# Stores of the first two batches in two pieces, and the last leftover block copied by one engine

## The chip, the cores and the metric

The kernel runs on one core of a Trainium2 chip. The metric is device time in microseconds (us): 236.17 us, the median of three runs (236.04 to 236.21). The engines are named as in the profile: PE is TensorE, DVE is VectorE, ACT is ScalarE, POOL is GpSimd, and SP is SyncE, which here issues DMAs (transfers) and waits. DMAs are issued on three queues, those of SP, ACT and POOL.

## The reference

Attention over 32 learned memory slots in each of 8 batches and 8 heads (576 tokens, head size 64), followed by a gated feed-forward block over the 4,608 tokens. Cut to what matters:

```python
a = softmax(phi)                                  # over the tokens, 8 x 8 x 576 x 32
k_m, v_m = einsum("bhsm,bhsd->bhmd", a, k), einsum("bhsm,bhsd->bhmd", a, v)
x = softmax(q @ k_m.T / sqrt(64)) @ v_m           # 8 x 8 x 576 x 64
x = x.transpose(0, 2, 1, 3).reshape(4608, 512)
out = (silu(x @ w_gate) * (x @ w_val)) @ w_out    # d_ff = 1536, out is 4608 x 512 in float32
```

## The kernel before

**Tiling.** The batches are taken one after the other, the first two interleaved. For a batch the kernel forms the memory's keys and values, the normalised attention `t_A`, and `t_U`, the product of the memory's values with the gate and value weights. The hidden layer `t_h` then comes from `t_U` and `t_A` (line 508), with the SiLU on ACT (line 525) and the gating product on DVE (line 531).

The last matmul, hidden layer by `w_out`, is done per batch on 2 x 2 blocks with seven products in place of eight (`products`, line 681; the matmul itself is line 719). Of the 576 tokens of a batch it takes 512, as two groups of 256: group `n` of a batch holds every second token (`out_r`, line 65). The sums and differences of blocks that the seven products need are `t_S` and `t_Q` (POOL and DVE) and `t_T` (of the weights). The remaining 64 tokens of each batch, the leftover, are gathered for four batches at a time (`quad`), which makes one small problem of 2 x 2 blocks of 128 tokens by 256 columns.

**Results and stores.** The four blocks of a result are called c11, c12, c21 and c22. PE accumulates products in PSUM banks; ACT moves intermediate sums to SBUF (`keep`, line 740: `t_p`, `t_q`); DVE adds (line 749). For a batch:

- `c11` and `c12` (lines 756 and 766) fill the tile `o1`, the first group's 256 tokens x 512 columns, held as 128 partitions x 2 x 512; `c22` and `c21` (lines 762 and 771) fill `o2`, the second group's.
- `both` calls `store_block` (line 671), which issues one DMA on SP's queue: 256 tokens, 512 KB.
- The tiles `o1` and `o2` come from a pool of three buffers (tag `to`), so the fourth tile waits for the landing of the first one's store.

For the leftover, `leftover` (line 777) makes one block of 128 tokens x 256 columns: for c11, c22 and c12 DVE adds (line 789); for c21 the bank is only copied. The block holds 64 tokens of each of two batches, and so has two stores of 64 KB (`store_leftover`, line 677), the first on SP's queue. For the second quad, which ends the kernel (`end` is true), the second store goes on SP's queue for c11, on ACT's for c22, on POOL's for c12 and on ACT's for c21, and the copy of c21 is cut in two halves of 128 columns, one on DVE and one on ACT (lines 793 and 794).

**Order.** The program is written by hand (`manual_schedule`, line 62): each engine and each queue does its work in the order in which the code names it. The end of the kernel is the list of the second quad's products, in the order p1/c11, q6, p5, c22, c12, c21 (line 822), each followed at once by its operation. In PE's last 1.5 us these are the product for c22, the one for c12 and the one for c21, six matmuls each. After that there is only the program's closing part, which the profile puts at line 1108: SP waits for all semaphores, and all engines meet in a barrier.

**Waits.** The framework that builds the program gives each DMA of SP's and ACT's queues one of eight semaphores in turn, and each DMA of POOL's queue one of eight others. A DMA waits for the one that had its semaphore before it. An instruction that waits for more semaphores than it can name itself has waiting rows (events) ahead of it.

Of the kernel before, what the change touches and what calls it, by code (L numbers as in the profile page):

```python
# [14 lines left out]
def kernel(  # L15
# [19 lines left out]
    nc = tc.nc  # L35
# [29 lines left out]
    out_r = out.rearrange("(b t r) c -> b r t c", b=B, r=2)  # L65
# [15 lines left out]
    def done(*tiles):  # L81

        for t in tiles:
            free.append(held.pop(id(t))[0])
# [243 lines left out]
    def copy(eng, out, in_):  # L328
        if eng == "a":
            nc.scalar.copy(out=out, in_=in_)  # L330
        else:
            nc.vector.tensor_copy(out=out, in_=in_)
# [337 lines left out]

    def store_block(t_o, b, n, cols):

        nc.sync.dma_start(
            out=out_r[b, n, 0:256, cols].rearrange("(u t) c -> t u c", u=2), in_=t_o[:, :, cols]
        )

    def store_leftover(t_o, b, cols, eng):

        eng.dma_start(out=out_b[b, 512:S, cols], in_=t_o)

    def products(b, by_hand, quad=None):

        h = DM // 2
# [3 lines left out]
        end = quad == 1 or (quad is None and b + 1 == B)  # L687
# [65 lines left out]
        def both(name, t0, cols):  # L753
            store_block(mine[name], b, t0 // 256, cols)
# [20 lines left out]
            both("o2", 256, slice(0, DM))  # L775

        def leftover(name, room, half, cols):
            other = dict(c22=nc.scalar, c12=nc.gpsimd, c21=nc.scalar) if end else {}
            engs = (nc.sync, other.get(name, nc.sync))

            def run():
                if room:
                    t = mine[room, "all"][:, half]
                else:
                    t = work.tile([128, h], FP32, tag="to", name="t_o")
                home = mine[dict(c11="a", c12="c").get(name, "s")]
                other = dict(c11="p1", c22="p5", c12="q6").get(name)
                if other:
                    nc.vector.tensor_tensor(
                        out=t, in0=home[:, 0], in1=mine[other][:, 0], op=ALU.add  # L790
                    )
                elif end:
                    copy("v", t[:, 0:h // 2], home[:, 0, 0:h // 2])
                    copy("a", t[:, h // 2:h], home[:, 0, h // 2:h])
                else:
                    copy("a", t, home[:, 0])
                if name != "c22":
                    done(home)
                for k in range(2):
                    x = 4 * quad + 2 * (name > "c20") + k  # L800
                    store_leftover(t[64 * k:64 * k + 64], x, cols, engs[k])

            return run
# [3 lines left out]
            c11=c11, c22=c22, c12=c12, c21=c21,  # L807
        )
        if quad is not None:
            ops.update(  # L810
                c11=leftover("c11", None, 0, lo), c12=leftover("c12", "q6", 1, hi),
                c22=leftover("c22", "p5", 1, hi), c21=leftover("c21", "q6", 0, lo),
            )
# [299 lines left out]
```

## Time and profile before

| | |
|---|---|
| median of the runs | 236.17 us (236.04 to 236.21) |
| the profiled execution | 236.21 us |
| its span, first to last instruction | 234.3 us |
| PE busy | 223.9 us (96%) |
| DVE, ACT, POOL busy | 183.1, 173.9, 141.1 us |
| granted TensorE clock | 1.00 throughout |
| DMA traffic | 36.84 MB, mean 157 GB/s |
| last matmul ends | 229.54 us |
| last DMA is issued | 230.24 us |

The span is what the trace shows; the run's own time is 1.9 us longer. A row of an engine gives the time in which it was busy; where an engine is idle, the profile names what released it. DMA issues and event rows are not counted as busy. The stores of `o1` and `o2`:

```profile
out_dram<-t_o SPq DMA_DIRECT2D x15, 512.0 KB, 3.6
```

These are 15 stores of 512 KB on SP's queue, with a median of 3.6 us from issue to landing. The four stores of batches 0 and 1 are issued between 67.6 and 77.8 us.

### The profile page before, as it was taken

The page shows a single profiled execution, that of the slowest core. Times are in us where ns is not written, and L with a number is a line of the kernel's source. Part 1 is how long each engine was busy: PE and PEld are TensorE (multiplying, and loading weights), DVE is VectorE, ACT ScalarE, POOL GpSimd, SP SyncE. Part 2 cuts the span into 40 slices and gives each one's busy share as a digit, 9 for nine tenths or more (in the row PEclk, how much of TensorE's full clock was granted, in tenths as well). Part 3 has the DMA queues.
Part 4 walks back from the last instruction along what each step waited for, and adds up shares of the span by engine and source line. Part 5 has one row for each costly group of instructions (what it writes and reads, how often), then busy time and mean ns, then how long its engine had stood idle before and what let it go on. Part 6 is the DMA issues. An engine that isn't in the chain of part 4 may idle for free.

```text
span 234.3 us, 7203 instructions
## 1 busy us (share of the span) xinstructions
PE 223.9 (96%) x2825; PEld 169.7 (72%) x2825; DVE 183.1 (78%) x421; ACT 173.9 (74%) x370; POOL 141.1 (60%) x191
## 2 busy tenths in 40 slices
PE   7987799999999999999999999999999999999991
PEld 2544466778887776878788787878788778878881
DVE  4155799999966698989797757989799879987631
ACT  2778799988547899968896758968897888777210
POOL 8422536997199059666967678465745484048490
PEclk9999999999999999999999999999999999999999
DMA  6999999999996992999199946993014602211224
GB/s 212 210 211 205 199 207 207 235 233 265 205 235 145 259 250 39 239 230 139 43 262 220 176 121 126 253 232 73 23 69 114 101 0 94 90 50 43 67 86 120
DMA packets 36562, 36.84 MB, mean 157 GB/s; under 512 B 14560, under 2 KB 30880, under 8 KB 36528
## 3 DMA queue, kind: packets, MB, share of 16 engines
q0 software_dynamic: 16304, 22.48, 51.6%
q1 hardware_dynamic: 19536, 13.18, 23.2%
q10 hardware_dynamic: 688, 0.72, 1.0%
q8 instruction: 22, 0.36, 0.6%
q14 instruction: 12, 0.10, 0.1%
HBM read 42.47 MB, written 9.44 MB: 222 GB/s over the span
## 4 chain that ended last, share of the span: by engine, by line
PE 86%; DMA 8%; POOL 2%; ACT 1%; issue 1%; DVE 0%; POOLq 0%; ACTq 0%
PE p_v L508 21%; PE p_g L508 21%; PE p_os L719 20%; PE p_oc L719 10%; DMA W<-in_moe_w_gate_dram 8%; PE p_u L465 5%; PE p_oa L719 5%; PE p_kv L230 2%; PE p_g L389 1%; POOL t_kv L99 1%; POOL t_kv L103 1%; PE p_q L376 0%; POOL t_q L108 0%; ACT t_qT L330 0%; PE p_kv L258 0%
## 5 line engine op out<-in xcount | busy, mean ns | idle before, releaser
L531 DVE TENSOR_TENSOR t_h<-t_sg,p_v 128x288 bf16<-128x288 bf16 x192 | 81.8, 451 | 17.6 <-PE p_v L508 7.6
L508 PEld LDWEIGHTS <-t_U 128*128 128x128 bf16 x768 | 73.6, 98 | 23.2 <-issue 3.8
L525 ACT ACTIVATE t_sg<-p_g 128x288 bf16<-128x288 f32 x192 | 74.0, 424 | 17.8 <-PE p_g L508 11.5
L508 PE MATMUL p_g<-t_A,t_U 128*128 128x288 bf16 x384 | 77.1, 286 | 0.5 <-ACT t_U L487 0.5
L508 PE MATMUL p_v<-t_A,t_U 128*128 128x288 bf16 x384 | 77.2, 286 | 0.0
L719 PEld LDWEIGHTS <-t_S 128*128 128x128 bf16 x384 | 37.5, 98 | 4.5 <-issue 0.2
L596 POOL TENSOR_TENSOR t_S<-t_h 128x512 bf16<-128x512 bf16 x17 | 19.6, 1155 | 32.7 <-DVE t_h L531 30.7
L719 PEld LDWEIGHTS <-t_h 128*128 128x128 bf16 x288 | 27.1, 98 | 8.6 <-issue 5.0
L485 ACT CAST t_U<-p_u 128x512 bf16<-128x512 f32 x53 | 28.0, 607 | 6.6 <-PE p_u L465 6.6
L719 PE MATMUL p_os<-t_T,t_S 128*128 128x256 bf16 x192 | 23.7, 273 | 0.0
L553 POOL TENSOR_TENSOR t_S<-t_S,t_h 128x512 bf16<-128x512 bf16 x17 | 19.6, 1154 | 1.3
L553 POOL TENSOR_TENSOR t_S<-t_h 128x512 bf16<-128x512 bf16 x16 | 18.4, 1152 | 0.0
L553 POOL TENSOR_TENSOR t_S<-t_h,t_S 128x512 bf16<-128x512 bf16 x16 | 18.4, 1151 | 0.0
L465 PE MATMUL p_u<-W,t_kT 64*32 64x512 bf16 (+1 forms) x416 | 15.8, 364 | 0.7 <-DMA W<-in_moe_w_gate_dram 0.7
L719 PE MATMUL p_os<-t_T,t_h 128*128 128x256 bf16 x96 | 14.8, 273 | 0.0
L870 PE MATMUL p_warm<-bones 128*128 128x512 bf16 x44 | 13.0, 435 | 1.7 <-DVE bones L892 1.7
L489 DVE CAST t_U<-p_u 128x512 bf16<-128x512 f32 x19 | 12.4, 682 | 1.9 <-PE p_u L465 1.9
L445 DVE TENSOR_TENSOR t_A<-t_E,t_lz 128x576 bf16<-128x576 bf16 x16 | 11.4, 739 | 0.7 <-ACT t_lz L421 0.7
L719 PE MATMUL p_oc<-t_T,t_S 128*128 128x256 bf16 x96 | 12.0, 273 | 0.0
L719 PE MATMUL p_oa<-WO,t_h 128*128 128x256 bf16 x96 | 11.8, 273 | 0.0
L719 PE MATMUL p_oc<-WO,t_S 128*128 128x256 bf16 x96 | 11.8, 272 | 0.1
L719 PE MATMUL p_os<-WO,t_h 128*128 128x256 bf16 x96 | 11.8, 272 | 0.0
(107 smaller groups left out, 309.3 us busy)
## 6 DMA issues: line engine op xcount, KB each, us to landing
out_dram<-t_o SPq DMA_DIRECT2D x15, 512.0 KB, 3.6
t_kv<-in_k_dram POOLq DMA_DIRECT2D x8, 576.0 KB, 10.6
t_q<-in_q_dram POOLq DMA_DIRECT2D x8, 576.0 KB, 8.7
t_kv<-in_v_dram POOLq DMA_DIRECT2D x8, 576.0 KB, 15.1
t_phi<-in_phi_dram POOLq DMA_DIRECT2D x6, 576.0 KB, 8.2
WO<-in_moe_w_out_dram POOLq DMA_DIRECT2D x3, 512.0 KB, 19.4
W<-in_moe_w_gate_dram POOLq DMA_DIRECT2D x2, 512.0 KB, 16.5
W<-in_moe_w_val_dram POOLq DMA_DIRECT2D x2, 512.0 KB, 16.0
```

What stands on the lines that cost most here:

```text
L230: nc.tensor.matmul(p[g][32 * i:32 * i + 32, 0:n], lhsT=phi_of(b, g, j, i), rhs=kvs[b][64 * g:64 * g + 64, w0:w1, i, j * D:(j + 1) * D], st ...
L445: nc.vector.tensor_tensor(out=a, in0=es.pop((b, g)), in1=lzs.pop((b, g)), op=ALU.mult)
L465: nc.tensor.matmul(p[g][32 * i:32 * i + 32, o:o + n], lhsT=kTs[b][64 * g:64 * g + 64, 2, 32 * i:32 * i + 32], rhs=w_part(w, c, i, g, halve ...
L485: nc.scalar.copy(out=t, in_=p)
L489: nc.vector.tensor_copy(out=t, in_=p)
L508: nc.tensor.matmul(p[:, 0:HALF], lhsT=Us[b, c, g][:, o // 2, which, 128 * (o % 2):128 * (o % 2 + 1)], rhs=atts[b, g][:, r], start=(g == 0) ...
L525: nc.scalar.activation(out=sg, in_=gate[:, 0:HALF], func=AF.Silu)
L531: nc.vector.tensor_tensor(out=dst, in0=sg, in1=val[:, 0:HALF], op=ALU.mult)
L553: eng.tensor_tensor(out=out, in0=x, in1=y, op=ALU.subtract)
L596: eng.tensor_tensor(out=t[:, 0], in0=A21, in1=A22, op=ALU.add)
L719: nc.tensor.matmul(mine[home][:, u], lhsT=lhs(c, m, u), rhs=rhs(c, m), start=fresh and u == 0, stop=(k == 5), skip_group_check=u == 1 or n ...
L870: nc.tensor.matmul(p[:, 0:128 * a], lhsT=bones, rhs=x.to_broadcast([128, a, 128]) if a > 1 else bones, start=True, stop=True,)
```

## The change

There are three edits.

1. `store_block`: for batches 0 and 1 the store of 256 tokens is issued as two DMAs of 128 tokens each, one after the other on SP's queue. Later batches keep one.
2. `leftover`, queue of the second store in the last quad: ACT for c22, c12 and c21, SP for c11. So c12's second store goes from POOL's queue to ACT's.
3. `leftover`, c21 of the last quad: DVE copies the whole block of 256 columns, in place of DVE and ACT half each.

```diff
     def store_block(t_o, b, n, cols):
-        nc.sync.dma_start(
-            out=out_r[b, n, 0:256, cols].rearrange("(u t) c -> t u c", u=2), in_=t_o[:, :, cols]
-        )
+        rows = out_r[b, n, 0:256, cols].rearrange("(u t) c -> t u c", u=2)
+        parts = [slice(u, u + 1) for u in range(2)] if b < 2 else [slice(0, 2)]
+        for u in parts:
+            nc.sync.dma_start(out=rows[:, u], in_=t_o[:, u, cols])
...
         def leftover(name, room, half, cols):
-            other = dict(c22=nc.scalar, c12=nc.gpsimd, c21=nc.scalar) if end else {}
-            engs = (nc.sync, other.get(name, nc.sync))
+            engs = (nc.sync, nc.scalar if end and name != "c11" else nc.sync)
...
-                elif end:
-                    copy("v", t[:, 0:h // 2], home[:, 0, 0:h // 2])
-                    copy("a", t[:, h // 2:h], home[:, 0, h // 2:h])
                 else:
-                    copy("a", t, home[:, 0])
+                    copy("v" if end else "a", t, home[:, 0])
```

## Prediction

> **What bounds the kernel now.** I read the page first, then busy time by stretch, then the end in order of time, the chain of work, the queues' waits, and last the trace's own records of semaphore updates. The rows of engines and slices come from the page:
>
> ```profile
> PE 223.9 (96%) x2825; PEld 169.7 (72%) x2825; DVE 183.1 (78%) x421; ACT 173.9 (74%) x370; POOL 141.1 (60%) x191
> ...
> PE   7987799999999999999999999999999999999991
> ...
> PEclk9999999999999999999999999999999999999999
> ```
>
> TensorE is busy almost without a break, at the full granted clock. The next lines split the span at the first store of a result (67.6 us), at the end of the last store of batches 0 and 1 (90), and at the last matmul's end (229.54). After the bounds come the length and then busy time (and count) of each engine.
>
> ```profile
> 67.60:90.00 22.40, 22.35 (x316) 16.96 (x315) 18.37 (x42) 16.92 (x37) 13.56 (x15) 1.00 0.92 219
> 90.00:217.00 127.00, 126.94 (x1572) 99.94 (x1570) 108.07 (x239) 104.23 (x226) 80.21 (x109) 1.00 0.59 125
> 217.00:229.54 12.54, 12.52 (x114) 10.88 (x112) 6.48 (x15) 2.50 (x5) 8.05 (x14) 1.00 0.29 95
> 229.54:234.30 4.76, 0.00 (x0) 0.00 (x0) 0.29 (x1) 0.27 (x1) 0.57 (x1) 1.00 0.35 84
> ```
>
> From 67.6 us to the last matmul TensorE idles 0.13 us in all, so a change outside TensorE's work can save next to nothing there; it can only add a stall. What is left is the last row: 4.76 us with no matmul, 2% of the span. The end in order of time (start, duration, engine, line):
>
> ```profile
> 226.20 0.69 DVE L332 COPY t_o<-p_os 128x512 f32<-128x512 f32 x1 [0.62 <-PE p_os L719]
> ...
> 228.68 0.47 SPq L679 DMA_DIRECT2D out_dram<-t_p  x1
> 228.69 0.55 ACTq L679 DMA_DIRECT2D out_dram<-t_p  x1
> 228.71 0.81 PE L719 MATMUL p_os<-t_T,t_x 128*128 128x256 bf16 x6
> 228.84 0.42 DVE L789 TENSOR_TENSOR t_q<-p_oc,t_q 128x256 f32<-128x256 f32 x1 [0.18 <-PE p_oc L719]
> 229.29 1.41 SPq L679 DMA_DIRECT2D out_dram<-t_q  x2
> 229.56 0.29 DVE L332 COPY t_q<-p_os 128x128 f32<-128x128 f32 x1 [0.30 <-PE p_os L719]
> 229.56 0.57 POOL L679 DMA_DIRECT2D out_dram<-t_q  x1 [1.36 <-DVE t_q L789]
> 229.94 0.27 ACT L330 COPY t_q<-p_os 128x128 f32<-128x128 f32 x1 [2.00 <-DVE t_q L332]
> 230.24 0.50 ACTq L679 DMA_DIRECT2D out_dram<-t_q  x1
> ```
>
> The two halves of the last copy do not run side by side: ScalarE's starts after VectorE's is done, and its row names that as the releaser. Only then do the last two stores go out, on SP and ACT. The waits of SP's queue from 230.5 us on:
>
> ```profile
> SPq L1108 <- DMA out_dram<-t_q: 1.6, 2, 1.1
> SPq L1108 <- PEq L1108: 0.7, 2, 0.5
> ```
>
> SP has a list of final waits at L1108, before the closing barrier. The trace's event rows give it step by step. Every DMA on SP's or ACT's queue marks its landing on one of eight semaphores, taken in turn (H0 to H7); those of POOL's queue have eight others (W0 to W7). Times are from the span's start:
>
> | SP passes the row at | the row waits for | which was complete at |
> |---|---|---|
> | 231.289 | H0 (SP's store of c12), W6 | 231.272 |
> | 232.466 | H1 (ACT's store of c21), W5 | 232.449 |
> | 232.530 | H2 (SP's store of c21), W4 | 232.189 |
> | 232.625, 232.700, 232.770 | H3 W3, H4 W2, H5 W1 (POOL's store of c12) | 231.771 at the latest |
> | 233.257 | H6 (ACT's store of c22), W0 | 230.916 |
> | 233.341 | H7 (SP's store of c22), ACT | 230.651 |
> | 233.411, 233.486 | POOL; then SP reports to the barrier | long before |
>
> The end of the span, 234.258, comes 0.772 after that report. So the last landing (232.449) is met in the second of nine rows, and 1.020 us pass from 232.466 to 233.486 in rows whose semaphores are full already: seven steps of 0.06 to 0.10 us and one of 0.49, for which no update and no transfer in the trace stands. I take it for a stall of SP itself.
>
> **The change part by part.**
>
> *Last block copied by VectorE alone.* Removed: 0.29 us of VectorE and, behind it, 0.27 of ScalarE with its hand-over. Added: one 128x256 copy. Rows of the same copy: 0.290 for 128 columns, 0.69 for 512 (above), so 0.00104 us a column and 0.423 for 256; the 128x256 additions also take 0.42. It starts at 229.563, as now, since it waits for the same matmul, and ends at 229.986; its semaphore is seen 0.01 later. The built order shows that SP and ACT then wait in an event row ahead of the DMA; such rows (the transposes of SP's queue) let their DMA start 0.03 us after. So the issue is at 230.045 against 230.236: **0.19 us earlier**.
>
> *Stores of c12.* The second half moves from POOL's queue to ACT's. POOL loses a 0.57 us issue and the 2.8 us drain behind it (229.540 to 232.356); the barrier waits for POOL's drain, but it ends before SP reports, so this is worth 0. ACT gains a wait for VectorE's addition (ends 229.265, so 229.29) and an issue of 0.50 to 0.57, till 229.86 at most. Behind it on ACT stands only the store of c21, which can't start before 230.045: 0.18 us of cover. Landing: ACT's two 64 KB stores were complete 2.228 and 2.213 us after issue, SP's three 1.967, 1.980 and 1.957. The new c12 store lands at 229.29 + 2.22 = 231.51, c21 at 230.045 + 2.213 = 232.258 (ACT) and 232.00 (SP). ACT's is the last, as now.
>
> The Trainium skill ("DMA: Bandwidth & Descriptors", section "Issuing engines are not separate DMA queues") says that stores from any engine end up on the same 16 engines and that the choice saves only issue time. By it the ACT store would land with SP's, 0.25 us sooner, and the total be 235.0; the five rows differ by queue, and I take the rows.
>
> *Four stores become eight.* They are issued at 67.61, 70.18, 74.29 and 77.80 with 0.37 us each (0.58 the first). SP gains four issues of 0.37 plus 0.05 between, 1.7 us. Behind them on SP stands the store of batch 2 (100.94) and a transpose (101.43), so over 20 us cover them. Bytes and the 2 KB pieces stay. VectorE and ScalarE get an extra event row in about seven places, since they wait for two landings per buffer: 0.06 us each, on engines that are 70 to 80% busy: 0. The nearest reuse of a buffer is at 74.845 (VectorE, c22 of batch 1), whose store was complete at 72.579, 2.27 us before. The second half is issued 0.6 later, so I expect 73.2 and no wait. Lower bound: 0, as TensorE has 0.05 us of idle time there to give back. Upper bound: the half lands as late after issue as the slowest of the four whole stores (77.80 to 87.23, 9.43 us), at 77.67, 2.8 us too late. I take 0, the value nearest to the row of that very store (4.96 us).
>
> The Trainium skill (same page, "Anatomy of one DMA — SWDGE (gpsimd) path") speaks against the split with a fixed cost of about 2 us per DMA, whatever its size. Were four of these on the path, it would be +8 us and 244; the stretch's 0.05 us of TensorE idle time puts none there.
>
> *What the split moves besides.* Semaphores go in turn, so four more DMAs shift every later one by four; ACT's added store shifts the last two by a fifth. The built order confirms it: c22 H2 (ACT) and H3 (SP), c12 H4 and H5, c21 **H6 (ACT) and H7 (SP)**. The final list keeps its order: (W7 W6), (H0 W5), (H1 W4), (H2 W3), (H3 W2), (H4 W1), (H5 W0), (H6 DVE), (H7 ACT), POOL, report. So the rows that now follow the last landing are passed before it. Up to H5 SP is through by 231.51 (ACT's c12) plus 0.1; H6 is complete at 232.258. The 0.49 us stall fits in that 0.65 us, wherever ahead of H6 it falls; SP's list begins six rows later in its program, which puts the stall, if it sits at a fixed place, still earlier. Behind H6: 0.017 to pass, 0.084, 0.070 and 0.075 as now, so the report is at 232.504 against 233.486.
>
> *The sum.* 0.19 (issue) + 0.79 (1.020 of rows behind the last landing become 0.229) = 0.98 us. Span 234.26 − 0.98 = 233.28. The profiled execution took 236.21, 1.9 around its span; the runs' median is 236.17, so 0.04 less: 235.19, **235.2 us**, −0.41%.
>
> **The rivals.**
>
> 1. *The stall comes after the last landing.* If 0.49 us belong to the last rows (SP slow after a long wait, say), 0.42 of them above a normal step stay: saving 0.56 to 0.49, **235.7**. For it: I have one sample and no cause. Against: now it comes five rows after the long wait, with normal rows between.
> 2. *The list isn't what holds the end*: the barrier waits for something else, so only the earlier issue counts: 0.19, **236.0**. Against: SP's report is the last of those at L1108; PE, DVE, ACT and POOL had reported or drained by 232.356. It would also be this if ACT's issue of c12 ran long and delayed c21 (SP once took 1.5 us for an issue, at 134.09: till 230.85, landing 233.07, saving 0.17).
> 3. *Slower: the second half of batch 0's first store lands after 74.845.* VectorE waits in order, the bank of c22 stays full and TensorE, without slack, stops for as long. It decides from 2.27 us beyond the old landing; the upper bound of 2.8 us late gives 236.17 + 2.8 − 0.98 = **238.0**. For it: the DMA engines are 0.92 busy in this stretch. Against: the bytes are the same, and the half is issued 0.6 us after the first.
>
> **How the numbers follow.** About 0.2% (0.47 us) is what a measurement of this kernel can tell from no change. Chances: forecast 0.62 (235.0 to 235.4: landings vary by 0.25), rival 1 0.16, rival 2 0.12, rival 3 0.10. Faster holds the forecast and half of rival 1, which lies on the bound: 0.70. Same holds its other half and rival 2: 0.20. Slower is rival 3: 0.10. The range goes from 234.9 (ACT's store landing as soon as SP's, 0.25, and a little of the spread between runs) to 236.0 (rival 2).
>
> **What would show it.** One 128x256 copy of 0.42 us at the end and DMA issues at about 230.05 on both queues; SP's waits at L1108 with one long wait that ends at the last landing; span end 1.0 us after that landing instead of 1.81; TensorE busy 223.9 still and its last matmul at 229.5. I am wrong if the last matmul moves, if ACT's c21 is issued later than 230.1, or if more than 0.25 us lie between the last landing and SP's report.

## The result, and the profile after

The changed kernel takes 235.02 us (median of six runs, 234.82 to 235.12) against 236.06 for the kernel before (six runs, 235.83 to 236.21). The ratio is 0.9956, with a 95% interval of 0.9943 to 0.9969: 1.04 us less. The forecast was 235.2.

The profiled execution took 234.91 us, with a span of 233.13. The same three rows of the page as before:

```profile
PE 223.6 (96%) x2825; PEld 169.7 (73%) x2825; DVE 183.2 (79%) x421; ACT 173.6 (74%) x369; POOL 140.6 (60%) x190
...
PE   7987899999999999999999999999999999999993
...
PEclk9999999999999999999999999999999999999999
```

TensorE does the same work at the same clock. Now busy time by stretch, cut at the same places (the last matmul ends at 229.29 here):

```profile
67.60:90.00 22.40, 22.35 (x316) 16.98 (x314) 18.37 (x42) 16.96 (x37) 13.55 (x15) 1.00 0.90 216
90.00:217.00 127.00, 126.97 (x1573) 100.11 (x1572) 108.29 (x239) 104.19 (x226) 80.17 (x109) 1.00 0.60 125
217.00:229.30 12.30, 12.29 (x112) 10.66 (x110) 6.25 (x14) 2.50 (x5) 8.04 (x14) 1.00 0.29 97
229.30:233.20 3.90, 0.00 (x0) 0.00 (x0) 0.42 (x1) 0.00 (x0) 0.00 (x0) 1.00 0.44 103
```

Where the split stores run (67.6 to 90), TensorE idles 0.05 us, as it did. The last row is what changed: 3.9 us behind the last matmul in place of 4.76. The end in order of time:

```profile
226.69 0.37 SPq L676 DMA_DIRECT2D out_dram<-t_o  x1
...
228.45 0.47 SPq L680 DMA_DIRECT2D out_dram<-t_p  x1
228.45 0.55 ACTq L680 DMA_DIRECT2D out_dram<-t_p  x1
228.48 0.82 PE L720 MATMUL p_os<-t_T,t_x 128*128 128x256 bf16 x6
228.61 0.42 DVE L789 TENSOR_TENSOR t_q<-p_oc,t_q 128x256 f32<-128x256 f32 x1 [0.18 <-PE p_oc L720]
229.06 1.24 SPq L680 DMA_DIRECT2D out_dram<-t_q  x2
229.10 1.39 ACTq L680 DMA_DIRECT2D out_dram<-t_q  x2
229.33 0.42 DVE L332 COPY t_q<-p_os 128x256 f32<-128x256 f32 x1 [0.30 <-PE p_os L720]
```

One copy of 0.42 us is the last work; ACT's half is gone. Rows that follow each other on a queue are merged here: "1.24, x2" on SP are the issues of c12 (229.059) and c21 (229.829), "1.39, x2" on ACT those of c12 (229.102) and c21 (229.966). The waits of SP's queue at the end:

```profile
SPq L1105 <- DMA out_dram<-t_q: 0.9, 2, 0.7
SPq L1105 <- PEq L1105: 0.7, 2, 0.5
```

The longest wait for a store fell from 1.1 to 0.7 us. The odd 0.5 us, for which the profile names an engine that had long been done, is still there; the trace's rows tell where. SP passes (W7 W6) at 230.340 and (H0 W5) at 230.828, so the gap of 0.46 us lies between these two now, ahead of every late landing. Then come H1, H2 and H3 in 0.22 us, H4 at 231.361, H5 at 231.423, H6 at 232.148 (complete at 232.131), H7 at 232.209, POOL at 232.274 and the report at 232.349.

### The profile page after: what moved, and what is told of

Read it like the earlier page. It is cut to its first block, busy times and chain, and to the rows that moved or that the text cites. A ratio compares the mean times of both kernels' runs of the same rounds, so it can differ in the third digit from the quotient of the medians.

```text
span 233.1 us, 7210 instructions
## 1 busy us (share of the span) xinstructions
PE 223.6 (96%) x2825; PEld 169.7 (73%) x2825; DVE 183.2 (79%) x421; ACT 173.6 (74%) x369; POOL 140.6 (60%) x190
## 4 chain that ended last, share of the span: by engine, by line
PE 88%; DMA 7%; POOL 1%; ACT 1%; DVE 1%; issue 1%; POOLq 0%
PE p_v L508 21%; PE p_g L508 21%; PE p_os L720 21%; PE p_oc L720 10%; DMA t_kv<-in_v_dram 7%; PE p_u L465 5%; PE p_oa L720 5%; PE p_kv L230 2%; PE p_g L389 1%; POOL t_kv L99 1%; PE p_mT L318 1%; PE p_warm L867 1%; PE p_q L376 0%; POOL t_q L108 0%; DVE t_kT L332 0%
```

## The experiments

Theory 1 is the prediction's: the end goes by the last landing and by the rows of SP's list of final waits that come behind it, and the split matters because it turns the semaphores. Theory 2: the early split gives TensorE or the transfers time back. Theory 3: the edits at the end carry the gain. The variants of theory 1 (1a: SP's stall sits at a fixed place of its program) are told in the expectations. From the second base on, the variants are measured in that base only, not on the changed kernel itself.

All readings of the end are in one table, from one profiled execution of each kernel. "Landing" is the time from the last matmul's end to the completion of the last store, "list" the time from there to SP's report to the barrier, "gap" the row of SP's program ahead of which its stall of 0.46 us stands, and "around" the run's own time less its span. The median is that of all runs of the kernel; the kernel before had 236.01 beside the first four experiments, 235.97 beside the next four and 235.79 beside the last four.

| kernel | last landing | landing | list | gap ahead of | span | around | median |
|---|---|---|---|---|---|---|---|
| before | H1 | 2.93 | 1.04 | H6 | 234.26 | 1.95 | 236.06 |
| changed | H6 | 2.84 | 0.22 | H0 | 233.13 | 1.78 | 235.02 |
| split only | H5 | 3.00 | 0.28 | H0 | 233.51 | 1.78 | 235.13 |
| edits at the end only | H2 | 2.75 | 0.97 | H6 | 233.78 | 1.90 | 235.78 |
| full turn | H3 | 3.04 | 0.39 | issue of c12 | 233.80 | 2.07 | 235.64 |
| split later | H6 | 2.79 | 0.21 | H2 | 233.63 | 1.90 | 235.05 |
| TensorE transposes: before | H0 | 2.92 | 0.57 | none | 240.29 | 1.79 | 241.99 |
| the same again | H0 | 2.91 | 0.57 | none | 239.93 | 1.79 | 241.77 |
| TensorE transposes: changed | H5 | 2.75 | 0.26 | none | 239.79 | 2.12 | 241.97 |
| the same again | H5 | 2.75 | 0.26 | none | 239.62 | 2.11 | 241.86 |
| ... one store of c21 | H7 | 5.33 | 0.14 | none | 242.13 | 1.98 | 244.29 |
| ... c12 on POOL | H5 | 2.72 | 0.26 | none | 239.86 | 2.11 | 241.93 |
| ... six batches split | H5 | 2.75 | 0.29 | second report | 240.15 | 1.89 | 241.66 |
| ... sixteen DMAs more | H5 | 3.55 | 0.27 | W7 W6 | 240.98 | 1.78 | 242.00 |

**Split only.** The new `store_block`; `leftover` as before.

```diff
+        parts = [slice(u, u + 1) for u in range(2)] if b < 2 else [slice(0, 2)]
+        for u in parts:
+            nc.sync.dma_start(out=rows[:, u], in_=t_o[:, u, cols])
```

> Only the split of the stores of batches 0 and 1; the end of the kernel as before. Theory 1 (the order of SP's final waits): the last stores are now on H5 (ACT) and H6 (SP), so after the last landing only the rows from H6 on remain, about 0.31 us to SP's report in place of 1.04, and SP's 0.46 us stall falls ahead of the H0 row, where it costs nothing: 0.73 us less, 235.35 against 236.06. Theory 2 (smaller stores early give TensorE time back): about as much as the whole change, 235.0, with TensorE's last matmul 0.2 us or more earlier. Theory 3 (the edits at the end carry it): no change, 236.06.

Measured 235.13, ratio 0.9961 (0.9948 to 0.9974): 0.88 us less, nearly the whole change from stores that are issued 150 us before the end. SP's waits:

```profile
SPq L1109 <- DMA out_dram<-t_q: 1.0, 1, 1.0
SPq L1109 <- PEq L1109: 0.7, 2, 0.5
```

One wait of 1.0 us for a store, late in the list, takes the place of two. The list fell from 1.04 to 0.28 us, as theory 1 has it (0.31), while the landing is as late as before. TensorE's last matmul is at 229.46, 0.06 earlier, so theory 2 has no such gain to show for it; theory 3 falls.

**Edits at the end only.** The old `store_block`; the new `leftover`.

> Only the edits of the last leftover block (one copy by DVE, c12's second store on ACT's queue); no store is split. Theory 1: the last stores are on H2 and H3, five rows and SP's stall (ahead of the H6 row) still come after the last landing; one row of 0.07 less than before, and 0.04 to 0.19 from the earlier issue and landing: 235.8 to 235.95. Theory 2: the same, as the split is missing, 235.8 to 236.0. Theory 3: most of the change, 235.0 to 235.3.

Measured 235.78, ratio 0.9990 (0.9982 to 0.9999): 0.23 less, within the bounds of theory 1 (0.11 to 0.26 less) and of theory 2, which had the same here; theory 3 falls again. The list is 0.97 us, with the gap ahead of H6, behind the last landing, and the landing 0.18 earlier.

**Full turn.** Eight more DMAs bring the semaphores round to where they were.

```diff
-        parts = [slice(u, u + 1) for u in range(2)] if b < 2 else [slice(0, 2)]
+        parts = [slice(u, u + 1) for u in range(2)] if b < 4 else [slice(0, 2)]
```

> The changed kernel with the stores of batches 2 and 3 split as well: eight more DMAs in place of four, which brings the semaphores once round, so the last stores are on H2 and H3 again. Theory 1: the rows H3 to H7, POOL and the report follow the last landing, 0.49 us in place of 0.22, but SP's stall (if it sits at a fixed place of its program) comes ahead of the last issue on SP and costs little: 0.27 us slower than the changed kernel, 235.3. Theory 2: as fast as the changed kernel or faster, 234.8 to 235.0. Theory 3: 235.0.

Measured 235.64, ratio 0.9985 (0.9977 to 0.9994). Twice the splits give little more than a third of the gain: theory 2 falls. Theory 1 had 235.3: its list was right in kind (0.39 us), but the gap came ahead of SP's issue of c12, which went out at 229.768, 0.35 behind ACT's, and SP's issue of c21 then took 0.84, so the landing is 0.2 later than in the changed kernel. I had priced that at nothing. The time around the span is longer too, 2.07 us in the profile and 1.83 to 2.09 in the twelve runs, where the six runs of the changed kernel have 1.77 to 1.82; why is open.

**Split later.** The same count of DMAs, 70 to 120 us later.

```diff
-        parts = [slice(u, u + 1) for u in range(2)] if b < 2 else [slice(0, 2)]
+        parts = [slice(u, u + 1) for u in range(2)] if b in (4, 5) else [slice(0, 2)]
```

> The changed kernel, but the four stores that are split are those of batches 4 and 5 in place of 0 and 1: the same number of DMAs, so the last stores are on H6 and H7 as in the changed kernel. Theory 1: as the changed kernel, 235.0, with SP's stall ahead of the H2 row, before the last landing. Theory 2: the early traffic is as before, so as the edits at the end alone, 235.8 to 236.0.

Measured 235.05, ratio 0.9956 (0.9942 to 0.9970): the whole gain. What the split does, it does by its number of DMAs and not by what it does to batches 0 and 1. Theory 2 is out. In these kernels the number of DMAs moves two things together, the rows behind the last landing and the place of the gap.

**A second base.** The first four kernels leave two things open: whether the shorter list is worth its time without the gap, and what the two edits at the end do apart. In this base TensorE does all transposes of queries and keys; SP issues nine DMAs fewer, and its rows in the trace end (67 and 73 of them) before the place of the gap.

```diff
-        if b > 3:
-            nc.sync.dma_start_transpose(out=kTs[b], in_=t.rearrange("p n x -> p (n x)"))
-            return
...
-                load_qT(b + 1)
...
+            streams += [(q_items(b + 1, "vav"), 13, 17)]
```

> The kernel before, with all transposes of queries and keys done by TensorE and none by a DMA (about 100 more small matmuls, some 10 us more in all; it is the base for the next three, which share this). SP's program has 69 instructions in place of 88, and the last stores are on H0 (ACT) and H1 (SP), the first of the list. Theory 1: seven rows, POOL and the report follow the last landing, 0.60 us, and there is no 0.46 us stall, since SP's program ends ahead of its 82nd instruction. Rival (the stall belongs to the list or to SP's long wait): a step of 0.46 us shows in the list here as well.

> The changed kernel, with all transposes done by TensorE. The last stores are on H5 (ACT) and H6 (SP). Theory 1: 0.28 us from the last landing to SP's report in place of 0.60, and some 0.1 earlier landing: 0.4 us faster than the kernel before in the same form, with no stall to be hidden. Rival (the stall is what was saved): 0.1 us faster at most.

> The kernel before with TensorE's transposes once more, as the base on the chip of the next three. Its SP program has 69 instructions, so SP's 82nd comes in the program's closing part that runs behind the span. Expected as measured: a span of 240.3 and 1.79 us around it, 242.0.

> The changed kernel with TensorE's transposes once more. Its profile had a span 0.50 us shorter than the kernel before in this form, but 2.12 us around the span in place of 1.79, and the same time. Theory 1a (SP's stall comes seven instructions behind the span here and lengthens the closing part): again 2.1 around the span and 242.0. Theory 1c (the 0.3 us around the span vary from run to run): 1.8 in about half of the executions, and a profile may show it; 241.6 to 242.0.

In both pairs the list is 0.57 us against 0.26 and no step in it is longer than 0.07, as theory 1 has it (0.60 and 0.28); the landing is 0.16 to 0.18 earlier. So some 0.47 us went from the end of the span. **The time didn't follow**: 241.99 and 241.97, then 241.77 and 241.86. The time around the span, 1.79 for the one, is 2.12 and 2.11 for the other. It goes with the kernel and not with the run, which is against theory 1c: the eight runs of the one have 1.76 to 1.86, the eight of the other 2.07 to 2.17. Theory 1a's reason, SP's gap in the closing part, isn't shown, and what the trace has of that part speaks rather against it. There are no instruction rows behind the span, but there are semaphore updates: the last comes 1.90 us behind it in the base and 1.99 in the changed kernel, in both profiles of each. So 0.09 of the 0.33 us show there, and the same 1.99 comes with six batches split (below), where the gap lies inside the span and the time around it is 1.89. Most of the 0.33 us has no record, and its cause stays open. What the shorter list is worth in time without the gap is therefore not shown either.

**One store of c21**, on the last semaphore:

```diff
+                if end and name == "c21":
+                    nc.sync.dma_start(out=out_b[4 * quad + 2:4 * quad + 4, 512:S, cols], in_=t)
+                    return
```

> As the changed kernel with TensorE's transposes, but the two 64 KB stores of the last block are one of 128 KB on SP, and the stores of batch 2 are split too, so that this last store is on H7, the last of the list. Theory 1: the last landing is SP's, about 2.0 us after an issue that comes with SP's in the other kernel, in place of ACT's, which is issued 0.14 later and takes 2.17: 0.3 us less, and one row of 0.06 less behind it: 0.35 to 0.4 us faster than the changed kernel in this form. Rival (issue and landing grow with the number of rows): no faster.

Measured 244.29, 2.3 us slower than the changed kernel in this form, where theory 1 had 0.35 to 0.4 faster. SP's waits, and the longest among them:

```profile
SPq L1099 <- DMA out_dram<-t_q: 3.7, 2, 3.2
```

The store is issued at 236.403 and complete at 241.210, 4.8 us later, where 64 KB took 2.0. Its semaphore's record points to the reason: one step at 237.400 and then only two, at 241.177 and 241.210, where the store before it, of c12, has sixteen. I read this as two DMA engines at work; the 1 KB packets follow each other, one every 0.02 us, till 240.83. The Trainium skill says this ("DMA: Bandwidth & Descriptors", section "Why a DMA increments its semaphore by 16 and not by 1"): the number of engines is the largest up to 16 that divides the slowest dimension of both sides, and the semaphore is raised at once for the engines that are left out. Here the slowest dimension of the target is 2, the two batches. The trace agrees with both. The row of H7 behind the landing was saved, though: the list is the shortest, 0.14 us.

**c12 on POOL.** The queue of c12's second store as before; one store of batch 2 split as well, so that the last semaphores are the same.

```diff
-            engs = (nc.sync, nc.scalar if end and name != "c11" else nc.sync)
+            engs = (nc.sync, dict(c22=nc.scalar, c12=nc.gpsimd, c21=nc.scalar).get(name, nc.sync) if end else nc.sync)
```

> As the changed kernel with TensorE's transposes, but c12's second store stays on POOL's queue, and one store of batch 2 is split too, so that the last stores are on H5 and H6 in both. Theory 1: ACT's store of c21 isn't held up by the issue of c12, so it goes out 0.14 us earlier, with SP's: 0.1 us faster than the changed kernel in this form; POOL's drain of 2.8 us ends before SP's report. Rival (POOL's drain holds the barrier): slower than the changed kernel in this form.

Measured 241.93 (241.55 to 242.22) against 241.97; theory 1 had 0.1 faster, which these four runs can't tell from no difference, and the rival (slower) isn't seen. The issues of c12 and c21 on the three queues:

```profile
235.89 1.22 SPq L672 DMA_DIRECT2D out_dram<-t_q  x2
236.16 0.57 POOL L672 DMA_DIRECT2D out_dram<-t_q  x1 [1.34 <-DVE t_q L781]
236.66 0.49 ACTq L672 DMA_DIRECT2D out_dram<-t_q  x1
```

ACT's issue of c21 does come with SP's (236.659 and 236.645), but its store lands 2.18 us after issue in place of 2.07, so that 0.03 of the 0.14 are left. In this form, moving c12's store to ACT neither helps nor hurts by more than the spread of the runs.

**Six batches split**, eight DMAs more than with two (`b < 6` in place of `b < 2`):

> The changed kernel with TensorE's transposes and the stores of batches 0 to 5 split, eight more DMAs: the last stores are on H5 and H6 as in the kernel with four, but SP's program has 83 instructions, and the 82nd is SP's second report to the closing barrier. Theory 1a: the 0.46 us stall shows ahead of that report, the span is 0.4 us longer than with four split stores, the time around it 1.8: in all 242.05, 0.1 slower. Rival (no fixed place): as with four, and no gap there.

The gap is where theory 1a put it: SP's second report comes 0.459 us behind the row ahead of it, in the other kernels 0.075. From SP's first report to the end of the span it is 0.96 us in place of 0.77, so 0.20 of the gap is felt there. The time around the span fell to 1.89, and the median is 241.66 (241.26 to 242.04), not above the 241.86 of four split stores but 0.2 below, with ranges that overlap. I had expected 0.1 slower; the place is shown, the price in the total is not.

**Sixteen DMAs more** than with four split stores:

```diff
+        parts = [slice(u, u + 1) for u in range(2)] if b < 4 else [slice(0, 2)]
+        halves = [slice(0, 256), slice(256, 512)] if b < 3 else [cols]
...
+                eng = nc.scalar if (b, n, u.stop, f.stop) == (1, 1, 2, 512) else nc.sync
```

> The changed kernel with TensorE's transposes and sixteen more DMAs than with four split stores (the stores of batches 0 to 2 in quarters, those of batch 3 in halves, one quarter on ACT's queue): the last stores are on H5 and H6 again, and SP's 82nd instruction is the first row of its final waits, ahead of the last landing. Theory 1a: the stall is hidden; span as with four split stores (0.26 us from the last landing to the report), 1.8 around it: 241.6, 0.3 us faster than with four. Rival (the place of the stall doesn't matter to the total): 242.0.

SP's gap is ahead of the first row, as expected, and 1.78 us lie around the span. But the median is 242.00 (241.61 to 242.75), the number that the rival had. The profiled execution is the slowest of the five. In it ACT's issue of c21 comes at 237.357, 0.34 us behind a waiting row that was done (0.04 in the other kernels), and its store lands 2.57 after issue (SP's 2.78); the last matmul ended 0.54 later than in the second profile with four split stores, a delay that was there by 20 us. A second stall, on ACT, is what that looks like; I have not tested it.

## Why the prediction was right

**What bounds the kernel**: right. TensorE idles in 0.13 us of 162 before the end, and the gain lies behind the last matmul.

**The list of final waits** was 0.79 us of the 0.98 and measured 0.82 (1.037 to 0.218, landing to report). The rows that were to be passed early were passed early, and the stall with them. The split alone took 0.76 off the list, and which batches are split didn't matter. This was the step that decided, and the diff doesn't say it: only the built program's semaphores do. How much of it is the stall (some 0.4 us) and how much the rows (as much again) is read from the rows of one profile; no pair of runs separates the two in the total.

**SP's stall** "at a fixed place": right. In the kernel before, the changed one and the six others that show it, it stands ahead of the 80th of SP's rows in the trace, whatever that row is. (The built program has two instructions more than the trace has rows, so the expectations call it the 82nd.) Rival 1 falls. What it is stays open. From 0.6 to 0.9 us behind each gap the trace has a transfer of 8 KB of instructions (before: gap till 233.257, transfer at 233.910; changed: 230.828 and 231.6), so I take it for SP's step from one block of its program to the next; no run shows that the transfer is SP's. The Trainium skill has blocks of 16 KiB and calls that step mostly hidden ("Runtime: NRT & Kernel Launch", section "Instruction fetch mechanics"); if that is what it is, it shows here with 0.46 us, of which some 0.4 is more than a normal step.

**The earlier issue** was the term that was mis-sized: 0.19 us expected, 0.04 found. The copy took 0.423 as worked out and SP issued 0.077 behind it, so SP's own store went out 0.17 earlier against the last matmul. The last landing is ACT's, though, and ACT's issue of c12 took 0.747 where I allowed 0.57 at most, from the rows in which ACT issues its first store of the end; so the 0.18 us of cover were used up, and ACT's store of c21 went out 0.14 behind SP's (229.966). In each of the nine profiles with c12's second store on ACT, its issue took 0.736 to 0.755, for instance with the edits at the end alone ("1.40, x2" is 0.748 for c12 and 0.531 for c21):

```profile
229.07 1.22 SPq L679 DMA_DIRECT2D out_dram<-t_q  x2
229.11 1.40 ACTq L679 DMA_DIRECT2D out_dram<-t_q  x2
```

SP's issue of c12 begins 0.04 us ahead of it, but that order isn't the reason, since in the full turn ACT's took 0.755 with SP's 0.35 behind it; the reason stays open. Rival 2's side case, an issue on ACT that runs long, came true in part. **The landing** gave 0.05 back (2.165 us after issue, 2.213 before).

**The signs of being wrong.** Two of the three came in substance. The last matmul moved: its row ends at 229.29 in place of 229.52, for the reason given below. ACT's c21 was issued at 229.97, ahead of the 230.1 of the sign, but only because the last matmul was 0.23 earlier; on the old clock that is 230.20. The third (more than 0.25 us from the last landing to SP's report) did not come: 0.22. One small slip of the sum: with ACT's store landing 0.25 us sooner it gives 234.9, not 235.0.

**What I did not forecast.** The profiled executions differ by 1.30 us: 0.82 of the list, 0.04 and 0.05 of issue and landing, 0.23 of TensorE and 0.17 around the span (and 0.01 lost in the barrier). Of TensorE's part 0.19 is this row of the kernel before, which has its like in the kernel with the split later; the other 0.04 is there by 33 us:

```profile
136.59 0.31 PEld L719 LDWEIGHTS <-t_Q 128*128 128x128 bf16 x3 [0.21 <-issue]
```

```profile
136.94 0.31 PEld L720 LDWEIGHTS <-t_Q 128*128 128x128 bf16 x3 [0.31 <-issue]
```

A weight load waits 0.2 to 0.3 us for nothing that the profile shows, at the same place of the program, in these two executions and in none of the changed kernel, the split alone, the edits at the end alone and the full turn. The split later, with as many DMAs as the changed kernel, has it; the edits at the end alone, with no store split, have not. So it does not go with the change. Without TensorE's 0.23 us the profiled pair comes to 1.07, beside 1.04 between the medians. The time around the span does go with the kernel: the six runs of the changed kernel have 1.77 to 1.82 us, the 23 of the kernel before that ran beside the first experiments 1.89 to 1.97. So some 0.13 us of the gain lie there, which I hadn't counted, and the earlier issue gave 0.15 us less than I had counted. That the total came so close is in part luck: the two nearly cancel.

**The split on the path** (rival 3): the two halves of the first store were complete at 70.406 and 72.100, the whole one at 72.579 before. The buffer's next use, at 74.8, was never near.

## What to carry to other kernels

When TensorE is busy to the last, look behind the last matmul: the order in which the closing waits are met against the order in which the last stores land. An edit that only changes the number of DMAs shifts which semaphore each later one gets, and can move the end without touching anything near it; count them in the built program before you credit the edit's own purpose. Read such a gain from the total as well as from the span, since in the second base 0.47 us less at the end of the span left the time as it was.

## What the runs showed of the hardware

- A store of 128 KB whose target has 2 as its slowest dimension took 4.8 us from issue to landing and ended with two semaphore steps; stores of 64 KB with sixteen steps took 2.0 on the same queue.
- SP's instruction stream has a gap of 0.46 us at a fixed place, ahead of the 80th of its rows in all eight kernels here that get that far. In the two whose list took about 1 us it lay behind the last landing, in the three whose list took 0.2 to 0.3 us and whose gain was largest ahead of it.
- A 64 KB store from ACT's queue was complete 2.07 to 2.29 us after issue at the end of these kernels, one from SP's queue 1.94 to 2.00 (the full turn and the kernel with sixteen DMAs more left out).
- The second of ACT's three issues at the end took 0.74 to 0.76 us, the first 0.55 and the third 0.48 to 0.54.
- The time around the span isn't a constant: from 1.78 to 2.12 us in the profiles. In the two kernels that were profiled twice it stays within 0.1 us over eight runs each (1.76 to 1.86 and 2.07 to 2.17); with c12 on POOL it went from 1.78 to 2.22 over four.
